# A copy moved from GpSimd to ScalarE and an earlier transpose in the last expert tiles of a fused attention and mixture-of-experts kernel

## The chip, the core and the metric

The kernel runs on one core of a Trainium2 chip. The core has five engines with a queue each, which work at the same time and meet only at semaphores: TensorE (PE in the profile, its weight loads PEld), VectorE (DVE), ScalarE (ACT), GpSimd (POOL) and SyncE (SP, which here starts DMAs). The metric is the device time of one execution in microseconds (us), lower is better. The time before is the median of three runs; the profile is of one further execution.

## The reference

Eight batches of eight heads of attention over 1152 keys, with neighbouring queries averaged in pairs, give 4608 rows of 512 numbers. Each row goes to one of eight experts, the one with the largest gate logit, and is weighted by two gates.

```python
q_pool = q.reshape(B, H, S // 2, 2, D).mean(axis=3)
scores = scale * np.matmul(q_pool, k.transpose(0, 1, 3, 2))
attn = softmax(scores); x = np.matmul(attn, v)          # then to 4608 x 512
...
e_idx = np.argmax(x @ w_gate, axis=1)
for e in range(8):
    mask = e_idx == e
    h = np.maximum(x[mask] @ w1[e], 0.0)
    out[mask] = gate_w[mask, None] * eom[mask, e, None] * (h @ w2[e])
```

Here w1 of an expert is 512 x 1024 and w2 is 1024 x 512, all in float32.

## The kernel before

The first two thirds of the time are attention, on all engines at once. The change does not touch it. Behind it `Moe.run` works through 22 expert tiles. A tile is a group of rows that one expert takes: tile -1 and the tiles 0 to 13 have 256 rows (kind D), tiles 14 to 17 have 192 (kind T), tiles 18 to 20 have 128 (kind S). A tail for more tiles stands behind a branch that is not taken here.

For precision a float32 matrix is held as a high part, rounded to the format of the matmul, and a low part, the rest. The product is then made of three products of parts. The steps of a tile t, with u the tile after it:

- `split1(u, c)`, c from 0 to 3: a quarter of the next w1. ACT copies the high part (L875), DVE subtracts for the low part (L876).
- `split2(t, g)`, g from 0 to 3: the same for w2 (L881, L882). S tiles leave it out and use w2 as loaded.
- `xt(u)`: PE transposes the gathered rows of the next tile (L892, one or two halves of four transposes), ACT copies the high part (L896), DVE subtracts for the low part (L897). X has two buffers, which tiles use by turns.
- `l1(t, g)`: a quarter of the first layer, 16 matmuls (L913). ACT and DVE add two parts of the sum (L915, L916), then ACT makes relu's high part hh (L922) and DVE the low part hl (L923). In S tiles it is one relu (L920).
- `l2(t, j)`: the second layer for rows 128 j to 128 j + 127. In D and T tiles each of eight chunks has three matmuls, hh with w2's high part (L943) and low part (L944) and hl with the high part (L946). In S tiles it is one matmul a chunk (L941), in 16 records for eight chunks. Then DVE scales the result by the gate (L957) and POOL scatters the rows (L958).
- `pack(t)`, only in T tiles: their second half has just 64 rows, so hl of these is copied into columns 192 to 255 of hh, beside hh's own 64. One 128-wide pass then does both, and l2(t, 1) has two matmuls a chunk. ACT and DVE add the two halves of its result (L953, L954).

The order on PE, DVE and ACT is written out by hand in `tile_`: these engines take their work in the order in which the code issues it. POOL's and SP's order is left to a scheduler. In `tile_` come first the four quarters of layer one with the w2 splits, then the four w1 splits of the next tile, then `pack(t)`, `l2(t, 0)`, `xt(u)` and, in D and T tiles, `l2(t, 1)`. On POOL stand, beside the copy of `pack`, the gathers of row numbers (L739) and of rows (L750) for a tile three ahead, and the scatters of results.

Of the kernel before, what the change touches and what calls it, by code (L numbers as in the profile page):

```python
# [8 lines left out]
F32 = mybir.dt.float32  # L9
# [704 lines left out]
class Moe:  # L714
# [79 lines left out]
    def run(self):  # L794
        tc, k, P1, NT = self.tc, self.keep, self.P1, self.NT
        nc = tc.nc
        V = nc.vector
        with ExitStack() as ctx:
# [38 lines left out]
            def slot(t):  # L837
                if t < 0:
                    return 'D', t
                return kinds[t] if t < NU else rest[t - NU]  # L840

            def width(t):
                return WIDTH[slot(t)[0]]

            def halves(t):
                return 1 if slot(t)[0] == 'S' else 2
# [19 lines left out]
            def loads(t, **kw):  # L866
                with tc.issue_after(lastw[0].ins):
                    e = nc.sync.value_load(z['ei'][0:1, t:t + 1], min_val=0, max_val=7)
                    c = nc.sync.value_load(z['chg'][0:1, t:t + 1], min_val=0, max_val=1)
                    lastw[0] = wload((t + 1) % 2, bass.ds(e, 1), cond=c, cond_hint=False, **kw)  # L870

            def split1(t, c, eng=V):
                raw = raw1[(t + 1) % 2]
                z = slice(256 * c, 256 * c + 256)
                nc.scalar.copy(out=W1[0][c], in_=raw[:, :, z])  # L875
                eng.tensor_tensor(out=W1[1][c], in0=raw[:, :, z], in1=W1[0][c].bitcast(F32), op=ALU.subtract)  # L876

            def split2(t, c):
                z = slice(2 * c, 2 * c + 2)
                raw = raw2[(t + 1) % 2]  # L880
                nc.scalar.copy(out=W2[0][:, z], in_=raw[:, z])  # L881
                V.tensor_tensor(out=W2[1][:, z], in0=raw[:, z], in1=W2[0].bitcast(F32)[:, z], op=ALU.subtract)  # L882

            def xt(t):

                d = T_[t]
                x = d['x'] = X[(t + P1) % 2]
                w = width(t)
                for j in range(halves(t)):
                    xp = ps_x.tile([128, 4, 128], F32, name="xps")  # L890
                    for c in range(4):
                        nc.tensor.transpose(out=xp[:, c], in_=d['xg'][j][:, 128 * c:128 * c + 128], identity=ident)  # L892
                    m = min(128, w - 128 * j)
                    z = slice(128 * j, 128 * j + m)
                    xp = xp[:, :, 0:m]
                    nc.scalar.copy(out=x[:, :, z], in_=xp)  # L896
                    V.tensor_tensor(out=x[:, :, w + 128 * j:w + 128 * j + m], in0=xp, in1=x.bitcast(F32)[:, :, z], op=ALU.subtract)  # L897

            def l1(t, g):

                d = T_[t]
                d['hh'], d['hl'] = H
                hp = ps_h.tile([128, 2, 512], F32, name="hps")
                z = slice(2 * g, 2 * g + 2)
                w = width(t)
                hh, hl = d['hh'][:, z, 0:w], d['hl'][:, z, 0:w]

                for f in range(2):
                    fs = slice(128 * f, 128 * f + 128)
                    for c in range(4):  # L910
                        for l in (0, 1) if c == 0 else (1, 0):
                            n = w if l else 2 * w
                            nc.tensor.matmul(hp[:, f, 0:n], lhsT=W1[l][g][:, c, fs], rhs=d['x'][:, c, 0:n], start=c == 0 and l == 0, stop=c == 3 and l == 0)  # L913
                hs = m1.tile([128, 2, TS], F32, name="hs", bufs=2)[:, :, 0:w]
                nc.scalar.copy(out=hs, in_=hp[:, :, w:2 * w])  # L915
                V.tensor_tensor(out=hs, in0=hp[:, :, 0:w], in1=hs, op=ALU.add)  # L916

                def relu():
                    if halves(t) == 1:
                        nc.scalar.activation(out=HR[:, z], in_=hs, func=AF.Relu)  # L920
                        return
                    nc.scalar.activation(out=hh, in_=hs, func=AF.Relu)  # L922
                    V.scalar_tensor_tensor(out=hl, in0=hs, scalar=0.0, in1=hh.bitcast(F32), op0=ALU.max, op1=ALU.subtract)  # L923
                return relu

            def packed(t, j):
                return j == 1 and width(t) == 192

            def pack(t):
                if packed(t, 1):  # L930
                    hh, hl = H
                    nc.gpsimd.tensor_copy(out=hh[:, :, 192:256], in_=hl.bitcast(F32)[:, :, 128:192])

            def l2(t, j):

                d = T_[t]
                yp = ps_y.tile([128, 512], F32, name="yp", tag="yp")
                z = slice(128 * j, 128 * j + 128)
                for c in range(8):
                    if halves(t) == 1:  # L940
                        nc.tensor.matmul(yp, lhsT=HR[:, c], rhs=raw2[(t + 1) % 2][:, c], start=c == 0, stop=c == 7)  # L941
                        continue
                    nc.tensor.matmul(yp, lhsT=d['hh'][:, c, z], rhs=W2[0][:, c], start=c == 0, stop=False)  # L943
                    nc.tensor.matmul(yp, lhsT=d['hh'][:, c, z], rhs=W2[1][:, c], start=False, stop=packed(t, j) and c == 7)  # L944
                    if not packed(t, j):
                        nc.tensor.matmul(yp, lhsT=d['hl'][:, c, z], rhs=W2[0][:, c], start=False, stop=c == 7)  # L946
                p = 64 if packed(t, j) else 128

                def y():
                    yt = my.tile([128, 512], F32, name="y", bufs=4)[0:p]  # L950
                    g = d['xg'][j][0:p, 512:513]
                    if p == 64:
                        nc.scalar.copy(out=yt, in_=yp[64:128])  # L953
                        V.tensor_tensor(out=yt, in0=yp[0:64], in1=yt, op=ALU.add)  # L954
                        nc.gpsimd.tensor_scalar(out=yt, in0=yt, scalar1=g, scalar2=1.0, op0=ALU.mult, op1=ALU.mult)
                    else:
                        V.tensor_scalar(out=yt, in0=yp, scalar1=g, scalar2=None, op0=ALU.mult)  # L957
                    nc.gpsimd.indirect_dma_start(  # L958
                        out=self.out, out_offset=bass.IndirectOffsetOnAxis(ap=d['ids'][j][0:p, 0:1], axis=0),
                        in_=yt, in_offset=None, bounds_check=self.NTOK - 1, oob_is_err=False)  # L960
                return y
# [116 lines left out]
            def gid(t):  # L1078
                if t < NL[0]:
                    kind, i = slot(t)  # L1080
                    self.gather_ids(t, z['ri' + kind][:, i], m1, 4)

            def gat(t):
                if t < NL[0]:
                    self.gather(t, mg, 3, self.NTOK + 1)
# [13 lines left out]
            def tile_(i, t, u):  # L1099

                acts = []
                for g in range(4):
                    if halves(t) > 1:
                        with tc.issue_after(self.exps[-1]):
                            split2(t, g)
                    if acts:
                        acts.pop(0)()
                    if g == 0 and pend:
                        pend.pop(0)()
                    acts.append(l1(t, g))  # L1110
                    if halves(t) == 1:
                        acts.pop(0)()
                    if todo:
                        todo.pop(0)()
                if t + 2 < NU and halves(t) > 1:
                    loads(t + 2, **(dict(behind=z['lg']) if t < 0 else {}))
                gid(t + 3)
                for c in range(4):
                    if u is not None:
                        split1(u, c)  # L1120
                    if acts:
                        acts.pop(0)()
                    next(late, None)
                pack(t)
                pend.append(l2(t, 0))
                if t + 2 < NU and halves(t) == 1:
                    loads(t + 2)
                gat(t + 3)
                pend.pop(0)()
                if u is not None:  # L1130
                    xt(u)
                if halves(t) > 1:
                    pend.append(l2(t, 1))
# [105 lines left out]
```

## Time and profile before

| | |
|---|---|
| three runs | 1510.71, 1520.57 and 1522.30 us, median 1520.57 |
| the profiled execution | 1513.06 us, its span 1511.2 us |
| granted PE clock over the span | 0.993 of full speed |
| span of the tiles 14 to 20 | from 1376.94 us to the end at 1511.2 us |

The times of rows are counted from the start of the span. A row of a timeline has a start, a length, the engine, the line, the operation, what it writes and reads, a count, and in brackets how long the engine stood idle before it and what ended that wait. Neighbouring instructions of a kind are merged into one row with a count. Matmuls overlap, so the length of a PE row is longer than what it adds: the distance of two starts says more.

### The profile page before, as it was taken

To read this page: it belongs to the slowest core of one execution; us is meant where nothing else is said; L and a number is where in the kernel's file an instruction comes from. 1 tells how busy PE (TensorE), PEld (TensorE's weight loads), DVE (VectorE), ACT (ScalarE), POOL (GpSimd) and SP (SyncE) were. 2 spreads that over 40 slices of the span, in tenths; PEclk is the share of its full clock that TensorE was granted. 3 is DMA by queue.
4 is the path that set the end of the run, shared out by engine and by line. 5 is a ranking of instruction groups with operands and counts; after the bars stand their busy time and mean duration, and the time that the engine had idled before them with its cause. 6 is when DMAs were issued, how large, how long until landed. Compare 5 with 4: busy or idle time off the path is not lost.

```text
span 1511.2 us, 40875 instructions
## 1 busy us (share of the span) xinstructions
PE 1463.8 (97%) x15806; PEld 1332.1 (88%) x15806; DVE 1100.5 (73%) x2359; ACT 1120.6 (74%) x1953; POOL 1021.0 (68%) x900
## 2 busy tenths in 40 slices
PE   7999999999999999999999999987999999999997
PEld 6999999999999999999999899976888888888885
DVE  7677777777777777777778677737877777777762
ACT  5788888888888888888888888884655655556652
POOL 4887888788888889888888988787233333333420
PEclk9999999999999999999999999998999999999999
DMA  5577566675576556665567556357966666357661
GB/s 170 135 187 179 144 167 149 162 180 122 146 175 165 140 136 171 167 153 152 139 164 181 144 149 162 78 191 261 336 229 242 227 215 238 136 210 242 234 219 41
DMA packets 96659, 265.95 MB, mean 176 GB/s; under 512 B 12778, under 2 KB 17018, under 8 KB 96450
## 3 DMA queue, kind: packets, MB, share of 16 engines
q1 hardware_dynamic: 85994, 241.52, 56.9%
q0 software_dynamic: 9024, 20.85, 3.9%
q8 instruction: 128, 2.10, 0.6%
q10 hardware_dynamic: 1440, 0.89, 0.2%
q14 instruction: 73, 0.60, 0.1%
HBM read 164.23 MB, written 22.50 MB: 124 GB/s over the span
## 4 chain that ended last, share of the span: by engine, by line
PE 90%; DVE 5%; ACT 2%; issue 1%; POOL 1%; DMA 1%; ACTq 0%; POOLq 0%; DVEq 0%; SPq 0%
PE mp L330 20%; PE hps L913 14%; PE sps L393 11%; PE sps L395 10%; PE av L424 6%; PE av L425 6%; PE av L426 6%; PE yp L943 4%; PE yp L944 4%; PE yp L946 4%; DVE pm L331 2%; PE yp L941 1%; PE tp L479 1%; PE xps L892 1%; PE tp L496 1%
## 5 line engine op out<-in xcount | busy, mean ns | idle before, releaser
L331 DVE TENSOR_REDUCE pm<-mp 128x1 f32<-128x384 f32 x864 | 452.5, 550 | 214.2 <-PE mp L330 213.3
L409 POOL TENSOR_TENSOR pl<-p,ph 128x576 f16<-128x576 f32 x386 | 494.4, 1287 | 146.7 <-ACT ph L408 110.7
L407 ACT ACTIVATE p<-sps 128x576 f32<-128x576 f32 x386 | 252.9, 655 | 98.5 <-PE sps L395 54.2
L330 PE MATMUL mp<-ka,qa 128*128 128x384 f32 x960 | 314.9, 344 | 0.0
L424 PEld LDWEIGHTS <-ph 128*128 128x128 f16 x2880 | 262.4, 97 | 39.6 <-issue 29.7
L424 PE MATMUL av<-vt,ph 128*128 128x65 f16 x2880 | 295.1, 194 | 0.0
L425 PE MATMUL av<-vt,ph 128*128 128x64 f16 x2880 | 293.0, 194 | 0.0
L426 PE MATMUL av<-vt,pl 128*128 128x65 f16 x2880 | 292.2, 192 | 0.0
L393 PE MATMUL sps<-qa,ka 128*128 128x288 f32 x1152 | 277.7, 322 | 12.6 <-ACT ph L408 7.3
L425 PEld LDWEIGHTS <-ph 128*128 128x128 f16 x2880 | 265.2, 97 | 0.8
L426 PEld LDWEIGHTS <-pl 128*128 128x128 f16 x2880 | 265.4, 99 | 0.0
L330 PE MATMUL mp<-kb,qb 66*128 66x384 f32 x768 | 261.0, 340 | 0.6 <-DVE kb L204 0.6
L408 ACT ACTIVATE ph<-sps 128x576 f16<-128x576 f32 x386 | 251.6, 652 | 0.0
L395 PE MATMUL sps<-qb,kb 68*128 68x288 f32 x1152 | 246.7, 296 | 0.0
L913 PE MATMUL hps<-x,w1h 128*128 128x512 f32 (+2 forms) x704 | 223.0, 381 | 4.2 <-DVE x L897 4.2
L393 PEld LDWEIGHTS sps<-qa,ka 128*128 128x128 f32 x1152 | 183.3, 190 | 18.0 <-ACT ph L408 10.8
L395 PEld LDWEIGHTS sps<-qb,kb 68*128 68x128 f32 x1152 | 185.5, 189 | 0.0
L330 PEld LDWEIGHTS mp<-ka,qa 128*128 128x128 f32 x960 | 178.4, 190 | 1.7 <-DVE pm L331 1.5
L913 PE MATMUL hps<-x,w1l 128*128 128x256 f32 (+2 forms) x704 | 162.3, 271 | 0.0
L915 ACT COPY hs<-hps 128x512 f32<-128x512 f32 (+2 forms) x88 | 47.4, 538 | 147.8 <-PE hps L913 135.6
L403 DVE TENSOR_TENSOR pl<-sps,ph 128x576 f16<-128x576 f32 x190 | 143.6, 756 | 18.2 <-ACT sps L400 15.6
L399 ACT ACTIVATE ph<-sps 128x576 f16<-128x576 f32 x190 | 124.4, 655 | 40.7 <-PE sps L395 30.7
(258 smaller groups left out, 2934.8 us busy)
## 6 DMA issues: line engine op xcount, KB each, us to landing
ka<-xk SPq DMA_DIRECT2D x120, 288.0 KB
raw1b<-in_w_dram SPq DMA_DIRECT2D x24, 1024.0 KB
raw2b<-in_w_dram SPq DMA_DIRECT2D x24, 1024.0 KB
raw1a<-in_w_dram SPq DMA_DIRECT2D x22, 1024.0 KB
raw2a<-in_w_dram SPq DMA_DIRECT2D x22, 1024.0 KB
vp<-in_vL_dram SPq DMA_DIRECT2D x32, 576.0 KB
qp<-in_qT_dram SPq DMA_DIRECT2D x31, 576.0 KB
kpf<-in_kT_dram SPq DMA_DIRECT2D x31, 576.0 KB
```

Of the source, the lines that this page charges most:

```text
L330: nc.tensor.matmul(mp, lhsT=l, rhs=r, start=j == 0, stop=j == len(ops) - 1)
L331: nc.vector.tensor_reduce(out=pm[:, i:i + 1], in_=mp, axis=AX.X, op=ALU.max)
L393: nc.tensor.matmul(sps[:, j, 0:288], lhsT=ka[:, h, ks], rhs=qa[:, o + 288 * j:o + 288 * j + 288], start=True, stop=False)
L395: nc.tensor.matmul(sps[:, j, 0:288], lhsT=kb[:, h, ks], rhs=qb[:, h, 288 * j:288 * j + 288], start=False, stop=True)
L403: nc.vector.tensor_tensor(out=pl.rearrange("p (j n) -> p j n", j=2), in0=x, in1=ph2, op=ALU.subtract)
L407: nc.scalar.activation(out=p32.rearrange("p (j n) -> p j n", j=2), in_=x, func=AF.Exp, scale=1.0 / 16)
L408: e_ = nc.scalar.activation(out=ph2, in_=x, func=AF.Exp, scale=1.0 / 16)
L409: nc.gpsimd.tensor_tensor(out=pl, in0=p32, in1=ph, op=ALU.subtract)
L424: nc.tensor.matmul(av_[:, qb, 0:65], lhsT=hi, rhs=vt[:, h, c, 0:65], start=c == 0 and qb == 0, stop=False)
L425: nc.tensor.matmul(av_[:, qb, 0:64], lhsT=hi, rhs=vt[:, h, c, 66:130], start=False, stop=False)
L426: nc.tensor.matmul(av_[:, qb, 0:65], lhsT=lo, rhs=vt[:, h, c, 0:65], start=False, stop=c == NC - 1 and qb == 4)
L913: nc.tensor.matmul(hp[:, f, 0:n], lhsT=W1[l][g][:, c, fs], rhs=d['x'][:, c, 0:n], start=c == 0 and l == 0, stop=c == 3 and l == 0)
```

## The change

The copy of `pack` is issued on ScalarE in place of GpSimd, and earlier: not behind all four w1 splits of the next tile but between the second and the third. In S tiles the next tile's x is transposed ahead of the second layer, in place of behind it. In D and T tiles `xt(u)` stays where it was.

```diff
@@ pack(t)
                 if packed(t, 1):
                     hh, hl = H
-                    nc.gpsimd.tensor_copy(out=hh[:, :, 192:256], in_=hl.bitcast(F32)[:, :, 128:192])
+                    nc.scalar.copy(out=hh[:, :, 192:256], in_=hl.bitcast(F32)[:, :, 128:192])
@@ tile_(i, t, u)
                 for c in range(4):
+                    if c == 2:
+                        pack(t)
                     if u is not None:
                         split1(u, c)
                     if acts:
                         acts.pop(0)()
                     next(late, None)
-                pack(t)
+                if u is not None and halves(t) == 1:
+                    xt(u)
                 pend.append(l2(t, 0))
                 if t + 2 < NU and halves(t) == 1:
                     loads(t + 2)
                 gat(t + 3)
                 pend.pop(0)()
-                if u is not None:
+                if u is not None and halves(t) > 1:
                     xt(u)
                 if halves(t) > 1:
                     pend.append(l2(t, 1))
```

How the rows of the engines' queues stand, before (-) and now (+). First ACT in tile 14, where the last relu of the tile and the four splits of w1 for tile 15 stand (raw1a is the loaded w1, w1h its high part):

```order
 L922 ACTIVATE hh<-hs 128x2x192
 L875 CAST w1h_22411<-raw1a 128x1024
+L932 CAST hh<-hl 128x8x64
 L875 CAST w1h_22412<-raw1a 128x1024
 L875 CAST w1h_22413<-raw1a 128x1024
```

The copy is new in ACT's queue, with two splits behind it. On POOL in the same tile, between a gather of row numbers and one of rows:

```order
 L958 DMA out_dram<-y,ids 4608x512
 L739 DMA ids<-idscr,riT 128x16
-L932 CAST hh<-hl 128x8x64
 L750 DMA xg<-xrows,ids 128x513
 L958 DMA out_dram<-y,ids 4608x512
```

Nothing else moves on POOL. PE between the first layers of tile 18 (x_22421) and tile 19 (x_22420); hr is relu's result in an S tile, raw2b its w2, xps the transposed rows of tile 19:

```order
 L913 MATMUL hps<-x_22421,w1l_22417 128x128
 L913 MATMUL hps<-x_22421,w1h_22413 128x256
+L892 MATMUL xps<-ident,xg 128x128 x4
 L941 MATMUL yp<-raw2b,hr 128x512 x8
-L892 MATMUL xps<-ident,xg 128x128 x4
 L913 MATMUL hps<-x_22420,w1h_22410 128x256
 L913 MATMUL hps<-x_22420,w1l_22414 128x128 x2
```

The four transposes move ahead of the second layer. DVE at the same place, behind the last w1 splits for tile 19:

```order
 L876 TENSOR_TENSOR w1l_22416<-raw1a,w1h_22412 128x1024
 L876 TENSOR_TENSOR w1l_22417<-raw1a,w1h_22413 128x1024
-L957 TENSOR_SCALAR y<-yp,xg 128x512
 L897 TENSOR_TENSOR x_22420<-xps,x_22420 128x4x128
+L957 TENSOR_SCALAR y<-yp,xg 128x512
 L916 TENSOR_TENSOR hs<-hps,hs 128x2x128 x4
```

The low part of x and the scaling of y change places; ACT's own order is the same there.

## The prediction

> **What bounds the kernel now.** I read the page's busy table first, then a windows view cut at the first matmul of each tile's first layer for the last seven expert tiles (the only ones that the change touches), then the waits of PE there, and last the timelines of single engines around each wait.
>
> ```profile
> PE 1463.8 (97%) x15806; PEld 1332.1 (88%) x15806; DVE 1100.5 (73%) x2359; ACT 1120.6 (74%) x1953; POOL 1021.0 (68%) x900
> ...
> 1376.94:1398.68 21.74, 19.50 (x114) 17.57 (x113) 15.71 (x20) 12.23 (x18) 9.26 (x7) 1.00 0.74 257
> 1398.68:1420.02 21.34, 19.46 (x113) 17.55 (x113) 15.94 (x20) 12.98 (x19) 10.03 (x8) 1.00 0.67 231
> 1420.02:1439.20 19.18, 19.18 (x113) 17.53 (x113) 16.25 (x20) 12.97 (x19) 8.83 (x7) 1.00 0.64 210
> 1439.20:1457.95 18.75, 18.75 (x110) 17.09 (x110) 14.52 (x18) 11.50 (x17) 5.54 (x5) 1.00 0.68 249
> 1457.95:1474.06 16.11, 14.71 (x86) 10.60 (x84) 8.39 (x11) 8.10 (x14) 2.42 (x3) 1.00 0.60 201
> 1474.06:1490.39 16.33, 14.93 (x84) 10.82 (x84) 7.77 (x10) 7.52 (x13) 0.93 (x2) 1.00 0.19 72
> ...
> PE yp L943 <- POOL hh L932: 4.1, 2, 2.2
> PE hps L913 <- DVE x L897: 2.8, 2, 1.4
> ```
>
> PE is the bound: 97% of the whole span, and in the windows (length, then busy time and count of PE, weight load, DVE, ACT and POOL, the clock, the DMA share) it fills tiles 16 and 17 entirely. Tiles 14 and 15 do the same work as 16 and take 21.74 and 21.34 us against 19.18. Tiles 18 and 19 leave PE idle 1.40 us each. The waits name what ends these holes: the copy at L932 twice, 4.1 us, and the low part of x at L897 twice, 2.8 us. Nothing else stops PE there, and the clock is 1.00. So about 7 us of some 1511 lie within the change's reach, under half a per cent: that is the frame of all that follows.
>
> **Part 1, the copy (tiles 14 to 17).** Removed: four casts on POOL. Added: four casts on ACT, between the second and the third split of the next w1. First what PE does at the place, in tiles 14, 15 and 16.
>
> ```profile
> 1391.44 1.03 PE L892 MATMUL xps<-ident,xg 128*128 128x128 f32 x8
> 1394.71 0.50 PE L943 MATMUL yp<-w2h,hh 128*128 128x512 f32 x1 [2.23 <-POOL hh L932]
> ...
> 1398.52 0.33 PE L913 MATMUL hps<-x,w1h 128*128 128x384 f32 x1
> ...
> 1413.18 1.03 PE L892 MATMUL xps<-ident,xg 128*128 128x128 f32 x8
> 1416.10 0.50 PE L943 MATMUL yp<-w2h,hh 128*128 128x512 f32 x1 [1.88 <-POOL hh L932]
> ...
> 1419.86 0.33 PE L913 MATMUL hps<-x,w1h 128*128 128x384 f32 x1
> ...
> 1434.52 1.04 PE L892 MATMUL xps<-ident,xg 128*128 128x128 f32 x8
> ...
> 1439.04 0.33 PE L913 MATMUL hps<-x,w1h 128*128 128x384 f32 x1
> ```
>
> From the first transpose to the next tile's first matmul takes 7.08 us in tile 14 (1398.52 - 1391.44), 6.68 in tile 15 and 4.52 in tile 16, where nothing is waited for. The hole is thus 2.56 and 2.16 us, 4.72 together; the windows give the same (21.74 - 19.18 and 21.34 - 19.18). Why the copy was late is on POOL's own timeline:
>
> ```profile
> 1393.01 1.02 POOL L739 DMA_INDIRECT ids<-idscr,riT  x1 [5.50 <-DVE w1l L876]
> 1394.04 0.62 POOL L932 CAST hh<-hl 128x512 fp32r<-128x512 f32 x1
> ...
> 1432.60 1.47 POOL L932 CAST hh<-hl 128x512 fp32r<-128x512 f32 x1 [1.83 <-DVE hl L923]
> ```
>
> In tile 14 the cast itself took 0.62 us, but it stood behind a gather of ids that did not start until 1393.01, after 5.5 idle us of POOL. In tile 16 no gather stood in front, and the cast ran as soon as hl was there, though it took 1.47. So the loss is the place in POOL's queue and not the length of the copy. [...]
>
> Now when the copy can run on ACT, and what it holds up there. It reads the last quarter of hl (DVE, L923) and stands ahead of two of ACT's four w1h splits; DVE's w1l splits follow them one for one, and after those come y and the low parts of x, for which the next tile's first matmul waits.
>
> ```profile
> 1366.70 0.63 ACT L922 ACTIVATE hh<-hs 128x512 fp32r<-128x512 f32 x1
> ...
> 1388.01 2.94 ACT L875 CAST w1h<-raw1a 128x1024 fp32r<-128x1024 f32 x3
> 1392.08 0.86 ACT L896 CAST x<-xps 128x512 fp32r<-128x512 f32 x2 [1.12 <-PE xps L892]
> ...
> 1388.84 0.55 DVE L923 SCALAR_TENSOR_TENSOR hl<-hs,hh 128x384 fp32r<-128x384 f32 x1
> 1389.31 3.49 DVE L876 TENSOR_TENSOR w1l<-raw1a,w1h 128x1024 fp32r<-128x1024 f32 x3
> 1392.71 0.74 DVE L957 TENSOR_SCALAR y<-yp,xg 128x512 f32<-128x512 f32 x1
> 1393.37 1.01 DVE L897 TENSOR_TENSOR x<-xps,x 128x512 fp32r<-128x512 f32 x2
> ...
> 1432.38 3.91 DVE L876 TENSOR_TENSOR w1l<-raw1a,w1h 128x1024 fp32r<-128x1024 f32 x3
> 1436.20 0.74 DVE L957 TENSOR_SCALAR y<-yp,xg 128x512 f32<-128x512 f32 x1
> 1436.86 1.01 DVE L897 TENSOR_TENSOR x<-xps,x 128x512 fp32r<-128x512 f32 x2
> ```
>
> The trace has no such copy on ACT. Its bounds: 0.63 us, an ACT pass of the same 128x512 from SBUF to fp32r (L922), and 1.47, the slowest cast of these very elements, on POOL. I take 0.63, since engine and size are the same and only the stride differs. In tile 14 hl is done at 1389.39 (1388.84 + 0.55), the copy then runs to about 1390.05, well ahead of 1392.2, where PE could use it (1391.44 + some 0.8 for the transposes). ACT has spent its second split by 1389.05 (a third of 2.94 is 0.98), waits 0.35 for hl and copies for 0.6: its third and fourth split end about 1.0 us later, the last at 1392.0 in place of 1390.95. ACT stood idle 1.12 us right behind them, waiting for the transposes, so L896 does not move. DVE's third w1l has to wait for the third w1h until 1391.0 and loses about 0.55 us; x is then ready at 1394.38 + 0.55 = 1394.9. The next layer can now start at 1391.44 + 4.52 = 1395.96, so 1.0 us of cover is left. With 1.47 us for the copy, x would come at 1395.8, still in time. If that cover went, each further microsecond of copy would cost one in each of the four tiles.
>
> Tiles 16 and 17 waited for nothing and can only lose. In tile 16 x was ready at 1437.87 and the next layer began at 1439.04, 1.17 us later. ACT's copy would push DVE by 0.55, but DVE's three splits took 3.91 us beside POOL's cast against 3.49 in tile 14, and about 0.4 of that comes back: x moves by some 0.15 us, hidden. Their cost: 0. What was queued behind the cast on POOL (gathers of x rows and scatters of y) comes earlier by the cast's length, and the order of its DMAs is otherwise as before; nobody waits for them at this point. Part 1: -4.72 us.
>
> **Part 2, x of the next tile ahead (tiles 18 and 19).** Four transposes change places with the 16 matmuls of the second layer on PE, and on DVE the low part of x with y; ACT's order does not change. The rows of tile 18, PE, then ACT, then DVE:
>
> ```profile
> 1465.19 7.03 PE L941 MATMUL yp<-raw2b,hr 128*128 128x512 f32 x16
> 1472.06 0.60 PE L892 MATMUL xps<-ident,xg 128*128 128x128 f32 x4
> 1474.06 0.39 PE L913 MATMUL hps<-x,w1h 128*128 128x256 f32 x1 [1.40 <-DVE x L897]
> ...
> 1466.63 3.87 ACT L875 CAST w1h<-raw1a 128x1024 fp32r<-128x1024 f32 x4
> 1472.70 0.58 ACT L896 CAST x<-xps 128x512 fp32r<-128x512 f32 x1 [2.19 <-PE xps L892]
> ...
> 1467.69 4.63 DVE L876 TENSOR_TENSOR w1l<-raw1a,w1h 128x1024 fp32r<-128x1024 f32 x4 [1.42 <-ACT w1h L875]
> 1472.26 0.75 DVE L957 TENSOR_SCALAR y<-yp,xg 128x512 f32<-128x512 f32 x1
> 1473.31 0.69 DVE L897 TENSOR_TENSOR x<-xps,x 128x512 fp32r<-128x512 f32 x1 [0.30 <-ACT x L896]
> ```
>
> Now the transposes end near 1465.7 and x's high part (ACT) follows the four splits: 1470.5 + 0.58 = 1471.1. Its low part needs DVE, which is busy with the four w1l splits until 1472.3 whatever PE does: it starts where y started, at 1472.26, and ends at 1472.95. PE has finished the second layer about 0.45 us later than before, near 1472.5 to 1472.7, so what is late next is DVE, and PE waits some 0.35 us for it. The next layer starts 0.06 after x, as before (1474.06 - 1474.00), at 1473.01. Gain 1.05 us, with 1.40 (the hole closed) as the upper bound and -0.45 (the transposes delay the second layer and x comes no sooner) as the lower; I take 1.05, because each row of its chain is known. y comes 0.7 us later, for which nobody waits in these tiles. Tile 19 has the same rows, tile 20 has no successor, and tile 17 before them keeps its old order. Part 2: 2 x -1.05 = -2.10 us.
>
> Loads do not step in, by two stretches of the windows view:
>
> ```profile
> 1464.00:1468.00 4.00, 4.00 (x19) 2.52 (x18) 1.15 (x3) 2.48 (x5) 0.96 (x1) 1.00 0.06 12
> ...
> 1480.00:1484.00 4.00, 4.00 (x21) 2.67 (x20) 0.85 (x2) 2.46 (x6) 0.00 (x0) 1.00 0.00 0
> ```
>
> The DMA share (last but one) is 0.06 from 1464 on: what was asked for till then, w1 of tile 20 as the last, had landed. Tile 20's first split comes as far into tile 19 as 1466.63 is into tile 18, near 1482.7, and 7 us earlier it is still 8 us behind that. W2 of tile 20, whose buffer the second layer of tile 18 frees, had landed by 1480, and its use begins 7.2 us (1465.19 - 1457.95) after 1490.39.
>
> **Sum.** -4.72 - 2.10 = -6.82 us. Against the profiled execution (1513.06 us, its span 1511.2, so 1.9 lie around it) that gives 1506.2, span 1504.4. The median of the three runs is 1520.57, 7.5 above the profiled one, and the runs go from 1510.71 to 1522.3; the change has nothing to do with that spread. I set the time at the median less the sum: 1513.8 us, 0.45% below.
>
> **Rivals.**
> - *ACT's copy becomes the bound, slower.* ACT works in order, so the copy holds two splits, DVE behind them and x behind DVE. It decides from a copy of about 1.6 us (0.63 plus the 1.0 of cover); at 3.3 us the four losses of 1.7 eat the whole 6.8, and at 4.0 the kernel is 4 x 2.4 - 6.8 = 2.8 slower: 1523.4. For it: DVE is busy 16 of 19 us in tile 16, with no slack to make good. Against it: the slowest pass over these elements in the trace took 1.47.
> - *The copy was not what PE waited for.* Had the second half of layer two waited for y's eviction by DVE (in tile 14 done at 1393.45, 1.2 us after PE was ready at 1392.2, and hardly earlier in tile 15), part 1 would gain only some 2.3 and the time be 1520.6 - 4.4 = 1516.2. Against it: in tile 16 that half had long begun when y ran at 1436.20, and in tile 14 it began 0.05 us after the cast's end.
> - *Only part 2 gains.* If the copy on ACT ends as late as on POOL (it waits for more than hl, so for a DVE step behind w1l), part 1 gives 0 and the time is 1518.5. For it: DVE works in order too, and a w1l split follows hl at once (1389.31). Against: POOL's copy in tile 16 started right behind hl, with the same wait.
>
> **How the numbers follow.** The forecast gets 0.80, as every step is in a row but the copy's length; the slower rival 0.06, the second 0.08, the third 0.06. The gain of the forecast, 5 to 7.5 us, is smaller than the spread of single runs (11.6 us), so the range follows the spread: from the lowest run less the sum, 1510.71 - 6.82 = 1503.9, up to the median without any gain, 1521. Faster or slower by more than 1%, 15 us, is about what a measurement of this kernel can tell from no change. Faster needs the medians to fall apart by another 8 us by luck: 0.10. Slower needs the first rival and bad luck: 0.03. The rest, 0.87, is within 1%.
>
> **What would show it.** Tiles 14 and 15 as long as tile 16, near 19.2 us; no wait of L943 for a copy; L932 on ACT at about 0.63 us, just behind hl, and L896 unmoved against its transposes; x of tiles 14 to 17 ready some 1 us ahead of its matmul; tiles 18 and 19 at 15.1 and 15.3 us with a wait for L897 of 0.3 to 0.4 in place of 1.40. I am wrong if L943 waits for ACT or DVE, if L913 waits for x in tiles 15 to 18, or if the last windows keep their length.

## The result, and the profile after

The changed kernel takes 1508.64 us (median of ten runs, 1502.54 to 1515.19), the kernel before 1519.47 (median of ten, 1510.15 to 1525.61). The ratio is 0.9949 with a 95% interval of 0.9929 to 0.9970: 7.7 us less, between 4.6 and 10.8. The plain difference of the two medians is 10.8 us, the upper end of that interval. That is a real gain and less than 1%. In a second set of runs the ratio was 0.9966 (0.9951 to 0.9981). The forecast was 6.8 us less, at 1513.8.

The windows view of the changed kernel, cut again at the first matmul of the tiles 14 to 20 (columns as in the prediction):

```profile
1384.42:1403.62 19.20, 19.20 (x114) 17.54 (x113) 15.70 (x20) 12.85 (x19) 8.13 (x6) 1.00 0.67 222
1403.62:1422.83 19.21, 19.21 (x113) 17.53 (x113) 15.87 (x20) 13.50 (x20) 8.42 (x7) 1.00 0.77 261
1422.83:1442.01 19.18, 19.18 (x114) 17.53 (x113) 15.95 (x21) 13.49 (x20) 8.76 (x8) 1.00 0.80 266
1442.01:1460.77 18.76, 18.76 (x111) 17.10 (x110) 14.52 (x19) 12.20 (x18) 4.40 (x4) 1.00 0.73 249
1460.77:1475.79 15.02, 14.70 (x84) 10.53 (x83) 7.66 (x11) 7.99 (x14) 1.65 (x2) 1.00 0.52 194
1475.79:1491.05 15.26, 14.94 (x84) 10.76 (x85) 7.59 (x11) 7.41 (x13) 1.01 (x1) 1.00 0.32 104
1491.05:1511.90 20.85, 14.54 (x80) 10.36 (x80) 3.05 (x6) 3.16 (x8) 1.96 (x2) 0.93 0.05 15
```

Tiles 14 and 15 are as long as tile 16, and PE is busy in all of their time. Tiles 18 and 19 went from 16.11 and 16.33 to 15.02 and 15.26. From the first layer of tile 14 to the end it is 127.48 us (1511.90 - 1384.42), before it was 134.26 (1511.2 - 1376.94): 6.78 less. Of the waits of PE in these tiles one kind is left, twice 0.32 us:

```profile
PE hps L913 <- DVE x L897: 0.6, 2, 0.3
```

ACT's timeline in tile 14 shows the copy where it now is, between the splits:

```profile
1395.49 1.04 ACT L875 CAST w1h<-raw1a 128x1024 fp32r<-128x1024 f32 x1
1396.90 0.63 ACT L932 CAST hh<-hl 128x512 fp32r<-128x512 f32 x1 [0.38 <-DVE hl L923]
1397.43 2.00 ACT L875 CAST w1h<-raw1a 128x1024 fp32r<-128x1024 f32 x2
1399.56 0.86 ACT L896 CAST x<-xps 128x512 fp32r<-128x512 f32 x2
```

And DVE's timeline there, with the last two low parts of w1, y and the low part of x:

```profile
1398.51 2.36 DVE L876 TENSOR_TENSOR w1l<-raw1a,w1h 128x1024 fp32r<-128x1024 f32 x2 [0.50 <-ACT w1h L875]
1400.79 0.74 DVE L957 TENSOR_SCALAR y<-yp,xg 128x512 f32<-128x512 f32 x1
1401.45 1.01 DVE L897 TENSOR_TENSOR x<-xps,x 128x512 fp32r<-128x512 f32 x2
```

ACT waits 0.38 us for hl, copies for 0.63, and DVE then waits 0.50 for the third high part of w1. L896 starts 0.64 us behind the start of PE's transposes, as before. x is ready at 1402.46, 1.0 us before PE takes it up: its timeline starts the next layer at 1403.46. The cut at 1403.62 is where the matmul before that one ends, since matmuls overlap by 0.16 us (a row is 0.39 us long, the next starts 0.23 us behind it). Behind the waits of 0.32 us in tiles 18 and 19 there is no such overlap, and the cuts at 1475.79 and 1491.05 are the starts of the matmuls themselves.

One thing in this profile looks wrong at first. Its span is 1511.9 us, longer than the 1511.2 of the profile before. All of that is ahead of the change: tile 14 begins at 1384.42 in place of 1376.94. Of these 7.5 us, 4.4 were there when the first expert layer began (at 1030.37 in place of 1025.95). PE's clock was lower for a while in this execution, in two of the first three stretches of 38 us (0.91, 0.96 and 0.91, where it had been 0.97, 0.94 and 1.00) and again around the first expert layer. The stretch around that layer, before and then after:

```profile
1026.00:1064.00 38.00, 35.13 (x176) 29.25 (x177) 29.88 (x69) 18.72 (x26) 23.87 (x20) 0.96 0.78 267
```

```profile
1026.00:1064.00 38.00, 31.37 (x141) 25.66 (x142) 28.23 (x77) 15.83 (x22) 25.96 (x21) 0.80 0.76 256
```

The granted clock was 0.80 there against 0.96. That the clock makes up all of the 7.5 us is not shown. Two single executions of this kernel differ by more than the change is worth, so the tiles were compared window by window and the whole by many runs.

### The profile page after: what moved, and what is told of

Read it like the earlier page. It is cut to its first block, busy times and chain, and to the rows that moved or that the text cites. A ratio compares the mean times of both kernels' runs of the same rounds, so it can differ in the third digit from the quotient of the medians.

```text
span 1511.9 us, 40870 instructions
## 1 busy us (share of the span) xinstructions
PE 1469.9 (97%) x15806; PEld 1338.4 (89%) x15806; DVE 1100.0 (73%) x2359; ACT 1123.7 (74%) x1957; POOL 1014.0 (67%) x896
## 3 DMA queue, kind: packets, MB, share of 16 engines
q0 software_dynamic: 9024, 20.85, 3.9%
## 4 chain that ended last, share of the span: by engine, by line
PE 91%; DVE 4%; ACT 2%; DMA 1%; POOL 1%; issue 1%; ACTq 0%; POOLq 0%; DVEq 0%; SPq 0%
PE mp L330 20%; PE hps L913 14%; PE sps L393 11%; PE sps L395 10%; PE av L424 6%; PE av L425 6%; PE av L426 6%; PE yp L943 4%; PE yp L944 4%; PE yp L946 4%; DVE pm L331 2%; PE tp L479 1%; PE xps L892 1%; PE tp L496 1%; PE yp L941 1%
```

## The experiments

The theory: in part 1 the cost was the copy's place in GpSimd's queue behind a gather, and in part 2 the transposes behind the second layer, with VectorE's splits as what comes late next. Rivals were the engine itself, the place among the splits, y's eviction, and a ScalarE that has no room for the copy.

**Each part alone.**

```diff
 part1_alone: the copy moved as in the change; xt(u) behind l2(t, 0) in all tiles
 part2_alone: xt(u) moved as in the change; the copy on nc.gpsimd behind the four splits
```

> Only the copy moves to ScalarE; x of the next tile stays behind the second layer in the 128-row tiles. Queue theory (the loss was the copy's place behind a gather in GpSimd's queue): tiles 14 and 15 fall from 21.7 and 21.3 to 19.2 us, tiles 18 and 19 stay at 16.1 and 16.3 with a wait of 1.40 for x; the time falls by 4.7 us, ratio 0.997. Theory that the second half of layer two waited for y's eviction: tiles 14 and 15 stay above 20.3.

> Only x of the next tile goes ahead of the second layer in the 128-row tiles; the copy stays on GpSimd behind the splits. Tiles 18 and 19 fall to 15.05 and 15.3 us with a wait for x of 0.3 us; tiles 14 and 15 keep a wait of 1.9 to 2.5 us for the copy. The time falls by 2.1 us, ratio 0.9986, less than the interval of five rounds. If the parts depend on each other, the falls of this and of part 1 alone do not add to 6.8.

Part 1 alone took 1512.79 us against 1516.71, ratio 0.9973 (0.9953 to 0.9993). Its windows for tiles 14, 15, 18 and 19:

```profile
1376.86:1396.06 19.20, 19.20 (x114) 17.54 (x113) 15.74 (x20) 12.85 (x19) 7.69 (x5) 1.00 0.66 221
1396.06:1415.27 19.21, 19.21 (x113) 17.53 (x113) 15.86 (x21) 13.48 (x20) 8.46 (x7) 1.00 0.74 261
...
1453.20:1469.31 16.11, 14.71 (x85) 10.60 (x83) 8.39 (x11) 8.10 (x14) 2.42 (x3) 1.00 0.55 203
1469.31:1485.64 16.33, 14.93 (x84) 10.82 (x84) 7.77 (x10) 7.51 (x13) 0.95 (x2) 1.00 0.19 73
```

Part 2 alone took 1513.00, ratio 0.9977 (0.9959 to 0.9994). Its windows for tiles 14 and 15 and a stretch inside tile 14, then tiles 18 and 19:

```profile
1374.74:1397.88 23.14, 21.06 (x113) 18.68 (x113) 15.71 (x20) 12.22 (x18) 9.34 (x7) 0.93 0.74 260
1397.88:1418.18 20.30, 19.47 (x114) 17.57 (x113) 15.96 (x20) 12.92 (x19) 9.84 (x8) 1.00 0.60 198
...
1394.00:1396.00 2.00, 2.00 (x7) 1.51 (x6) 1.23 (x1) 0.67 (x1) 0.82 (x1) 0.50 1.04 410
...
1456.11:1471.14 15.03, 14.71 (x85) 10.54 (x83) 7.67 (x11) 7.99 (x14) 1.66 (x2) 1.00 0.53 181
1471.14:1486.40 15.26, 14.94 (x84) 10.76 (x85) 7.59 (x11) 7.41 (x13) 0.99 (x1) 1.00 0.29 108
```

Each part closes its own holes and leaves the other's, and their intervals hold the 4.7 and 2.1 us of the sum. That the parts do not depend on each other rests on the windows; the times (4.1 and 3.5 us) are too coarse for it. Tiles 14 and 15 of part 2 were not as expected. Tile 14 took 23.14 us, more than before, with the clock at 0.50 behind a wait of 2.08 us; tile 15 waited only 0.83 us, where 1.9 at the least was expected. That was taken up by the last two runs.

**The copy on GpSimd, but first.**

```diff
-                    nc.gpsimd.tensor_copy(out=hh[:, :, 192:256], ...)
+                    return nc.gpsimd.tensor_copy(out=hh[:, :, 192:256], ...)
...
-                gid(t + 3)
                 for c in range(4):
...
-                pack(t)
+                pk = pack(t)
+                if pk is not None:
+                    with tc.issue_after(pk.ins):
+                        gid(t + 3)
+                else:
+                    gid(t + 3)
```

> The kernel before, with the copy still on GpSimd, but the gathers of row numbers for three tiles ahead are issued behind it in every tile that has it. Queue theory: the copy starts within 0.1 us of the end of the low part it reads, takes 0.6 to 1.5 us, and tiles 14 and 15 are at 19.2 us as on ScalarE. Engine theory (GpSimd is too slow or starts too late for this): a hole of more than 1 us stays in tiles 14 and 15. Tiles 18 and 19 keep 16.1 and 16.3.

The windows of tiles 14 and 15:

```profile
1383.81:1403.01 19.20, 19.20 (x114) 17.54 (x113) 16.03 (x20) 12.22 (x18) 8.00 (x6) 1.00 0.70 225
1403.01:1422.22 19.21, 19.21 (x113) 17.52 (x113) 15.97 (x20) 12.80 (x19) 9.41 (x8) 1.00 0.80 265
```

POOL's copy in tile 14 on its timeline:

```profile
1396.40 1.47 POOL L932 CAST hh<-hl 128x512 fp32r<-128x512 f32 x1 [6.63 <-DVE hl L923]
```

DVE's timeline there, with the last quarter of hl:

```profile
1395.71 0.55 DVE L923 SCALAR_TENSOR_TENSOR hl<-hs,hh 128x384 fp32r<-128x384 f32 x1
```

The holes close on GpSimd as well. The copy starts 0.14 us after hl ends (1395.71 + 0.55 = 1396.26), where 0.1 was expected, and is in time even at 1.47 us. So the engine was not the cause; the place in the queue was. The time of this single execution, 1515.22 us, says nothing about the whole, since its tile 14 began at 1383.81.

**The copy on ScalarE behind the four splits, and on VectorE.**

```diff
 act_copy_last:
                 for c in range(4):
-                    if c == 2:
-                        pack(t)
...
+                pack(t)
 dve_copy:
-                    nc.scalar.copy(out=hh[:, :, 192:256], ...)
+                    V.tensor_copy(out=hh[:, :, 192:256], ...)
```

> The changed kernel, with the copy on ScalarE behind all four splits of the next w1 in place of between the second and the third. Queue theory: it ends some 0.6 us behind the fourth split and still ahead of the end of the transposes, so tiles 14 and 15 stay at 19.2 us, and VectorE's splits no longer wait 0.5 us. Theory that the place ahead of two splits is needed: a wait of 0.5 us or more for the copy comes back in tiles 14 to 17.

> The changed kernel, with the copy on VectorE between the same splits. It stands right behind the low part it reads and needs no wait. Estimate of its length 0.4 to 0.75 us, from 0.55 for 128x384 and 0.75 for 128x512 on VectorE in the profile before. The splits and x behind it come that much later, inside the cover of 1.0 us: tiles 14 and 15 at 19.2 us, no wait for the copy or for x. If VectorE were the bound in these tiles, all four would be 0.4 to 0.7 us longer.

Behind the splits on ScalarE, the windows of tiles 14 and 15:

```profile
1379.62:1398.81 19.19, 19.19 (x113) 17.53 (x113) 15.63 (x20) 12.74 (x19) 8.21 (x5) 1.00 0.71 234
1398.81:1418.03 19.22, 19.22 (x114) 17.54 (x113) 15.90 (x20) 13.41 (x20) 9.03 (x8) 1.00 0.74 262
```

ACT's timeline in tile 14:

```profile
1393.52 0.62 ACT L932 CAST hh<-hl 128x512 fp32r<-128x512 f32 x1
1394.76 0.86 ACT L896 CAST x<-xps 128x512 fp32r<-128x512 f32 x2 [0.62 <-PE xps L892]
```

On VectorE, the windows of the same tiles:

```profile
1383.74:1402.93 19.19, 19.19 (x113) 17.53 (x113) 15.96 (x21) 12.24 (x18) 8.16 (x6) 1.00 0.67 219
1402.93:1422.14 19.21, 19.21 (x114) 17.53 (x113) 16.36 (x21) 12.95 (x19) 7.91 (x7) 1.00 0.78 270
```

DVE's timeline in tile 14:

```profile
1397.23 0.42 DVE L932 CAST hh<-hl 128x512 fp32r<-128x512 f32 x1
```

All four places end at 19.2 us a tile. On ScalarE behind the splits the copy fits into a stretch in which ACT would wait for PE's transposes anyway, and it still ends before they do (at 1394.14, and ACT then waits 0.62 us for them); VectorE's three splits take 3.49 us there, without a wait. The place among the splits, of which the change makes a point, is worth nothing here.

**How much room ScalarE has.**

```diff
 copy_twice, copy_four_times, copy_six_times (n = 2, 4, 6):
-                    nc.scalar.copy(out=hh[:, :, 192:256], ...)
+                    for _ in range(n):
+                        nc.scalar.copy(out=hh[:, :, 192:256], ...)
```

> The changed kernel with the copy on ScalarE made twice (the same columns again). Cover theory: the copies take 0.62 + 0.53 us, x is ready 0.5 us later and still 0.5 us ahead of its matmul; tiles 14 to 17 keep 19.2 and 18.8 us. Rival, that ScalarE's queue is already the bound there: each is 0.5 us longer.

> The changed kernel with the copy made four times, 2.2 us in all. Cover theory: x comes 1.6 us later, 0.6 behind the cover of 1.0, so each of tiles 14 to 17 is longer by about 0.6 us (19.8 and 19.4) and its first layer waits for the low part of x on VectorE. Rival, no such bound: unchanged.

> The changed kernel with the copy made six times, 3.3 us in all: the length at which the first rival put the break-even with the kernel before. Cover theory: x comes 2.65 us later, tiles 14 to 17 are each longer by about 1.65 us (20.8 and 20.4), so the seven tiles take 134.1 us as before the change (134.26). If it is less than half of that, the cover is larger than 1.0 us.

Two copies: tiles 14 to 17 at 19.19, 19.21, 19.18 and 18.76 us, as without. Four copies, windows of tiles 14 and 15 (the tiles 16 and 17 took 20.34 and 20.01), and PE's waits in the seven tiles, of which two are those of the tiles 18 and 19:

```profile
1377.21:1397.25 20.04, 19.19 (x113) 17.19 (x112) 14.63 (x20) 15.08 (x23) 8.35 (x5) 1.00 0.60 195
1397.25:1417.59 20.34, 19.51 (x112) 17.48 (x113) 15.55 (x21) 15.07 (x23) 7.81 (x8) 1.00 0.70 251
...
PE hps L913 <- DVE x L897: 3.9, 6, 0.9
```

Six copies, the windows of tiles 14 and 15 and PE's waits again:

```profile
1375.10:1396.44 21.34, 19.46 (x113) 17.22 (x112) 14.63 (x20) 16.32 (x25) 7.36 (x5) 1.00 0.53 183
1396.44:1418.08 21.64, 19.81 (x113) 17.51 (x113) 15.55 (x21) 16.30 (x25) 7.79 (x8) 1.00 0.70 237
...
PE hps L913 <- DVE x L897: 4.3, 6, 1.0
PE yp L944 <- ACT hh L933: 3.9, 4, 1.3
```

Their copies in tile 14, merged into one row of ACT's timeline:

```profile
1387.57 3.88 ACT L933 CAST hh<-hl 128x512 fp32r<-128x512 f32 x6 [0.38 <-DVE hl L923]
```

The copies cost 0.65 us each (3.88 / 6) and not 0.53, so the two longer runs lost more than was expected: by the windows 0.84 to 1.25 us a tile with four, 2.14 to 2.55 with six. What they say of the room is the same in both. It has to be read from the start of one first matmul to the next, since a window that ends in a wait and did not begin in one comes out 0.16 us short. So measured, tile 14 took 20.20 us with four copies (1397.25 - 1377.05) and 21.50 with six (1396.44 - 1374.94), against 19.20: of 3 x 0.65 = 1.95 us added 1.00 was lost, and of 3.25 us 2.30, which leaves 0.95 that cost nothing. In tile 15, 1.13 and 2.43 were lost, which leaves 0.82. In the changed kernel x is ready 1.00 us ahead of its matmul in tile 14 and 0.85 in tile 15, which agrees. The cover is 0.8 to 0.95 us.

With six copies PE also waits for the copies themselves, about 1 us in each of the tiles 14 to 17 (L944 for L933, which are L943 and L932 of the other kernels, one line down by the loop), ahead of its wait for x. That is a second way for a long copy to hold up PE, which the cover theory did not have. It adds nothing here, as x comes later still. With four the tiles 14 to 20 took 132.49 us (the span of 1509.7 less 1377.21), with six 137.30; on the line between, the 134.26 of the kernel before would be met at a copy of some 3.0 to 3.1 us.

**x between the splits.**

```diff
                 for c in range(4):
                     if c == 2:
                         pack(t)
+                        if u is not None and halves(t) == 1:
+                            xt(u)
...
-                if u is not None and halves(t) == 1:
-                    xt(u)
```

> The changed kernel; in the 128-row tiles the next x is made on ScalarE and VectorE between the second and the third split of the next w1 in place of behind the fourth. If VectorE's four low-part splits are what keeps 0.32 us of waiting in tiles 18 and 19, this wait goes: 14.70 and 14.94 us, 0.64 us in all, with TensorE busy without a hole from tile 14 to the last matmul. Against the kernel before 7.5 us, ratio 0.995. If the wait has another cause, it stays, or moves to the low parts of w1, which are ready 0.7 us later.

> The changed kernel once more, beside the version with x between the splits, on the same chip: ratio to the kernel before 0.995, tiles 14 to 20 as in its first profile (127.5 us from the first layer of tile 14 to the end) whatever the granted clock does ahead of them.

The version with x between the splits took 1507.04 us against 1514.88 for the kernel before on the same chip, ratio 0.9938 (0.9914 to 0.9962); the changed kernel beside it 1510.03, ratio 0.9966 (0.9951 to 0.9981). The windows of tiles 18 and 19 with x between the splits:

```profile
1456.14:1470.85 14.71, 14.71 (x86) 10.88 (x86) 7.35 (x10) 7.99 (x14) 1.65 (x2) 1.00 0.53 190
1470.85:1485.56 14.71, 14.71 (x86) 10.88 (x86) 7.59 (x11) 7.41 (x13) 1.01 (x1) 1.00 0.34 117
```

DVE's timeline in tile 18, x ahead of the last two low parts of w1:

```profile
1468.16 0.69 DVE L897 TENSOR_TENSOR x<-xps,x 128x512 fp32r<-128x512 f32 x1
1468.76 2.35 DVE L876 TENSOR_TENSOR w1l<-raw1a,w1h 128x1024 fp32r<-128x1024 f32 x2
```

The wait is gone. The high part of x on ScalarE had been ready 1.3 us before VectorE took it up in the changed kernel (1473.22 + 0.57 against 1475.06), so VectorE's splits were its cause. By the windows the two tiles gain 0.31 and 0.55 us. The 0.31 is 0.16 too small by the cut that was described above: from the start of one first matmul to the next tile 18 took 15.19 us in the changed kernel (1475.79 - 1460.60), so it gains 0.48. By its windows this version beats both kernels; by the times it beats the kernel before, and its interval overlaps that of the changed one. The repeat of the changed kernel took 19.20, 19.21, 19.18, 18.75, 15.03 and 15.26 us for tiles 14 to 19, the first profile's to 0.01. To the end it was 127.83 and not 127.5, the 0.35 being in the last window, 21.20 for 20.85. Its ratio was expected at 0.995.

**The holes once more.** Both kernels are repeats.

> The kernel before once more, for one look. If the holes in tiles 14 and 15 are fixed by the program, they are 2.6 and 2.2 us as in its first profile. If they depend on when the scatter ahead of the gather lands and on the granted clock behind the wait, as the profile of part 2 alone suggests (23.1 and 20.3 us there, with matmuls 0.43 us apart behind the first wait), they differ from that by 0.5 us or more, and their sum lies between 3 and 7 us.

> Part 2 alone once more, for one look. If its long tile 14 (23.1 us) comes from the program, it is there again. If it comes from the granted clock of that execution, tile 14 is at 21 to 22 us with matmuls 0.23 us apart behind the wait. Tiles 18 and 19 again at 15.0 and 15.3 us.

The kernel before, the windows of tiles 14 and 15:

```profile
1377.89:1399.64 21.75, 19.46 (x114) 17.57 (x113) 15.71 (x20) 12.23 (x18) 9.25 (x7) 1.00 0.71 256
1399.64:1418.83 19.19, 19.19 (x113) 17.50 (x113) 16.30 (x20) 12.95 (x19) 8.29 (x8) 1.00 0.61 203
```

POOL's gather of row numbers in tile 15, first in the earlier profile of this kernel and then in the repeat, and the repeat's copy, in time for PE here:

```profile
1414.14 1.29 POOL L739 DMA_INDIRECT ids<-idscr,riS  x1 [4.80 <-DMA out_dram<-y,ids]
...
1412.54 1.54 POOL L739 DMA_INDIRECT ids<-idscr,riS  x1 [4.44 <-DMA out_dram<-y,ids]
1414.10 0.70 POOL L932 CAST hh<-hl 128x512 fp32r<-128x512 f32 x1
```

Part 2 alone, the windows of the same tiles and a stretch behind the wait:

```profile
1377.07:1400.96 23.89, 21.07 (x113) 18.73 (x113) 15.71 (x20) 12.21 (x18) 9.40 (x7) 0.93 0.74 267
1400.96:1420.17 19.21, 19.21 (x113) 17.53 (x113) 15.96 (x20) 12.81 (x19) 7.96 (x8) 1.00 0.48 158
1396.00:1399.00 3.00, 3.00 (x9) 2.40 (x8) 1.22 (x1) 1.04 (x1) 1.58 (x2) 0.54 1.02 412
```

PE's wait in tile 14 on its timeline:

```profile
1395.42 0.50 PE L943 MATMUL yp<-w2h,hh 128*128 128x512 f32 x1 [2.82 <-POOL hh L932]
```

The holes are not fixed by the program. In the four profiles that have the copy behind the gather (the kernel before, its repeat, part 2 alone, its repeat) the hole in tile 14 was 2.56, 2.57, 3.96 and 4.71 us, the last two with the clock near 0.5 behind the wait. In tile 15 it was 2.16, 0, 1.12 and 0 us. Together they are 4.7, 2.6, 5.1 and 4.7 us; 2.6 is below the 3 that was expected at the least. Tiles 18 and 19 of part 2's repeat took 15.02 and 15.31 us, as expected.

In tile 15 the gather started 15.46 us into the tile in the first profile (1414.14 - 1398.68) and 12.90 us in the repeat, both times after a wait for a scatter of results. By the code that is the scatter which reads the row numbers that the gather is about to overwrite, as there are eight buffers for them and a tile of two halves uses two. In tile 14 the profile names a step of VectorE as what ended that wait in three of the four. No run moves the scatter or adds a buffer, so that the scatter's landing sets the size of the hole is read from the waits and not tested.

The long tile 14 came back in part 2's repeat, which the expectation read as a sign of the program; yet the matmuls in it run at about half the clock (0.54 in the stretch above, 0.50 in the one of the first profile), and up to there the program is that of the kernel before on PE, DVE, ACT and POOL. Why both executions of part 2 and none of the two of the kernel before had the slow clock stays open.

## Why the prediction was right

- *PE is the bound and 7 us are in reach.* Right. All places that closed the holes put tiles 14 and 15 at 19.2 us. With x between the splits the tiles 14 to 20 take 126.4 us, 7.9 less than before, a little over 7 since a wait cost more than its idle time here (2.23 us of wait were 2.56 of time in tile 14).
- *Part 1, 4.72 us, for the place in the queue.* Right in the cause, by the copy that stayed on GpSimd. The size was that of one execution: in four it was between 2.6 and 5.1, and 4.72 lies inside by luck as much as by reading. The prediction took the hole as a constant of the program and did not ask why POOL stood idle ahead of the gather; by the waits of tile 15 (4.80 and 4.44 us for a scatter in two profiles) that depends on when a scatter has landed.
- *The place in POOL's queue and not the length of the copy.* Right. The copy by itself took 0.62 us on POOL in tile 14 before and 0.62 on ACT, though VectorE did it in 0.42; on POOL it closed the hole even at 1.47 us, once it stood first.
- *The copy takes 0.63, hl holds it 0.35, DVE waits 0.55, 1.0 of cover is left.* Measured 0.62, 0.38, 0.50, and 0.8 to 0.95. For tile 16 the prediction let x move by 0.15 us; it moved by 0.35 (ready 0.82 us ahead of its matmul in place of 1.17), still hidden.
- *Part 2, 1.05 a tile, with 0.35 left behind DVE's splits.* Measured 1.09 and 1.07, with 0.32 left. The upper bound of 1.40, the idle time of the wait, was too low: with the wait closed the tiles gain 1.56 and 1.62 us from the start of one first matmul to the next.
- *The rival on ScalarE's room.* It does not come about, but its mechanism is real, as four and six copies show. The break-even was set at 3.3 us and is nearer 3.0.
- *The other two rivals,* y's eviction and a copy as late on ACT as on POOL. Both are excluded by part 1 alone, which put tiles 14 and 15 at 19.20 and 19.21 us.
- *The time.* The median fell by 10.8 us where 6.8 was set, and the ratio's interval, 4.6 to 10.8, holds the sum. The windows of two single profiles give 6.78, but this closeness is luck: the repeats of the same two kernels give 132.31 - 127.83 = 4.48 us for the tiles 14 to 20.

## What to carry to other kernels

When an engine waits for a small operation, look at what stands ahead of that operation in its own queue before blaming its engine: here the copy was as good on any of three engines, once nothing slow and unrelated stood in front of it. The gather of row numbers was such a thing here, and its start in tile 15 moved from 15.46 us into the tile to 12.90 from one execution to the next, so measure a hole in several profiles before giving it a price. After a wait is closed, ask which engine is late next; moving one step ahead of half of that engine's queued work took away the rest.

## What the runs showed of the hardware

- The waits on PE cost more than their idle time. Waits of 2.23 and 1.88 us made tiles 14 and 15 longer by 2.56 and 2.16, and closing the two waits of 0.32 gave 0.48 and 0.55 us. Two parts of this are in the rows. The overlap with what ran before is lost: 0.16 us with a matmul, 0.24 with the transposes (in tile 14 of the changed kernel their row starts at 1398.93 and is 1.03 us long, and the next matmul starts at 1399.72). And behind the wait in tile 14 the second matmul starts 0.35 us after the first (1395.06 - 1394.71), where without a wait it starts 0.31 after it (1400.03 - 1399.72).
- Behind waits of 2.08 and 2.82 us (tile 14 of part 2 alone and of its repeat) the granted clock fell to about half, 0.50 and 0.54 in the stretches above, and the matmuls started 0.43 us apart in place of 0.23 for some 3 us (1392.96 to 1395.95 and 1396.22 to 1399.62). Behind waits of 2.23 and 2.29 us (the kernel before and its repeat) it stayed at 1.00. So the length of the wait alone does not decide it; what does, no run here shows.
- The same cast on GpSimd took 0.62 and 0.61 us where it ran beside or just behind VectorE's low parts of x (L897, tiles 14 and 15 of the kernel before) and 1.47 us where it began 0.2 us into one of VectorE's splits (L876, tile 16). The next split then took 1.63 us in place of 1.22, so that three took 3.91 us in place of 3.49. With the copy first on GpSimd it began 0.23 us into the splits of tile 14 and took 1.47 us, and the three splits again took 3.91. In the repeat's tile 15 the cast took 0.70 us, and VectorE was busy for 16.30 us in that tile in place of 15.94.
- Copies back to back on ScalarE into the same columns take 0.65 us each (3.88 / 6 in tile 14 with six copies), while one before a split of other data adds 0.53 (1397.43 - 1396.90 in the changed kernel).
